# A hand-written order of 800 steps laid out anew around one shared port: attention and a two-layer network on one core

## The chip, the cores and the metric

The kernel runs on one core of a Trainium2 chip. The core has five engines with queues of their own: TensorE (PE, matmul; its weight loads are shown as PEld), VectorE (DVE), ScalarE (ACT), GpSimd (POOL) and SyncE (SP, which here issues all DMAs). The metric is the device time in microseconds (us); lower is better.

## The reference

Batch 4, 8 heads, 768 positions, head size 64. Each query sees the keys within 15 positions and, beside them, 24 block summaries (maximum of 32 keys, mean of 32 values, with log 32 added to the score). The result is the input of a network of two layers with a squared ReLU between them.

```python
k_sum = k.reshape(B, H, nb, block, D).max(axis=3)
v_sum = v.reshape(B, H, nb, block, D).mean(axis=3)
scores_l = scale * np.matmul(q, k.transpose(0, 1, 3, 2))
mask_l = np.abs(pos[:, None] - pos[None, :]) < window
scores_s = scale * np.einsum('bhsd,bhnd->bhsn', q, k_sum) + np.log(block)
scores_all = np.concatenate([np.where(mask_l, scores_l, -1e9), scores_s], axis=-1)
a = np.exp(scores_all - np.max(scores_all, axis=-1, keepdims=True))
a = a / (np.sum(a, axis=-1, keepdims=True) + 1e-09)
attn_out = np.matmul(a, np.concatenate([v, v_sum], axis=2))
...
x = attn_out.transpose(0, 2, 1, 3).reshape(B * S, H * D)   # 3072 x 512
h = np.maximum(x @ w_in, 0.0)                              # 512 -> 2048
return h * h @ w_out                                       # 2048 -> 512
```

## The kernel before

The attention is cut into 24 groups (4 batches x 6 tiles of 128 queries, all 8 heads), the network into 12 chunks of 256 rows, two groups each. The 2048 hidden units are 16 slices of 128; slice f has a weight tile that holds its part of both layers. Every float32 operand of the network is split into a rounded high part and a remainder (w high and low, xh and xl, gh and gl), and three products are added.

From chunk 2 on, a loop (`slot`, `period`) interleaves the network of one chunk with the attention of the next two groups. Ahead of it stands the head: groups 0 to 5, the whole preparation of the 16 weight tiles, and the network of chunks 0 and 1. The order of the head is written out by hand in the string `START`, one token for each step. The functions are called in the order of the tokens, so this string sets the order of the instructions in each engine's queue; the engines meet through semaphores. A token `TT2.5` means step TT for group 2, head 5; a letter at the end names the engine where there is a choice (a, v, p for ACT, DVE, POOL). The steps are:

- `L:x` a load on SP's queue (kv keys, q queries, vn and v values, w weights). Weight tile f goes into a room of the pool "w" (17 rooms, shared with keys and values), and its split copy w_sb takes another.
- `KS` block maxima (DVE); `S g.half` scores of four heads (PE, into banks 0 and 1 of PSUM); `TT` mask and maximum of one head (DVE); `E` exponential with its sum (ACT); `NR g.half` the inverse of four sums (DVE); `N` the multiplication by it (DVE or POOL); `T` transpose on PE, and `TC` its copy to SBUF.
- `SV` the block means of v on PE, `VC` their copies into the v tiles; `O g` outputs of group g (PE); `XH`, `XL` the split of x (ACT, DVE).
- For weight tile f: `HI` sign and scale (ACT), `LO` rounding (ACT or DVE), `SH` shift (DVE), `AD` add (POOL), `CA` high part (ACT or DVE), `SU` low part (DVE or POOL).
- `F1 u.j` a piece of the first layer (12 matmuls), `RE`, `SQ`, `MU`, `GL` the squared ReLU and its split (ACT or DVE, ACT, DVE, DVE), `F2 u.j` a piece of the second layer, `EV` the copy out. A unit u is a chunk and two slices; units 0 and 1 are chunk 0 with w0 to w3, units 2 to 5 chunk 1 with w0 to w7, and so on.
- `Wn`: n filler matmuls on zeros, whose results nobody reads.

The lines on which the steps rest: L164 KS, L263 S, L275 TT, L283 E, L293 and L296 NR, L301 N, L307 T, L110 every copy, L332 O, L346 and L349 XH and XL, L209 HI, L216 and L214 LO, L220 SH, L225 AD, L232 SU, L364 F1, L372 to L386 the squared ReLU, L410 F2, L543 fillers.

The mask-and-maximum reads scores from PSUM; the four sums of a half, `sm`, lie in SBUF.

Of the kernel before, what the change touches and what calls it, by code (L numbers as in the profile page):

```python
# [38 lines left out]


START = """
L:kv2 L:kv3 L:kv0 L:q0 L:mask L:kv1 L:w0 L:id L:q1 L:mean KS3 L:vn1 L:vn0 KS2 KS0 W7 S0.1 TT0.5 TT0.4 TT0.6 E0.4 TT0.7
KS1 E0.5 E0.7 E0.6 W3 S0.0 NR0.1 N0.1p L:q2 TT0.1 TT0.0 TT0.2 L:w1 E0.0 TT0.3 LO0v E0.1 L:v1 W3 T0.1 E0.3 L:v0 E0.2
S1.1 L:w2 HI0 NR0.0 S1.0 N0.0p TT1.4 TT1.7 TT1.6 TT1.5 E1.4 L:q3 SH0 E1.6 W1 T0.0 E1.7 AD0 TT1.1 TT1.2 TT1.0 E1.2
TC0.0v E1.0 E1.5 TT1.3 W6 SV E1.1 NR1.1 TC0.1v E1.3 N1.1p CA0a NR1.0 N1.0p S2.1 VC0v VC1a T1.1 VC2v SU0p VC3a T1.0
TC1.1a TT2.6 TT2.5 S2.0 TC1.0v HI1 L:q4 TT2.4 O1 TT2.0 TT2.7 E2.6 TT2.1 SH1 E2.7 O0 E2.0 LO1v E2.1 E2.5 L:v2 E2.4 CA1v
L:w3 XH1 NR2.1 AD1 L:w5 XH0 TT2.3 N2.1v L:v3 E2.3 L:w6 TT2.2 W8 T2.1 XL1 E2.2 L:w4 HI2 S3.0 NR2.0 SU1p N2.0v S3.1 LO2a
XL0 T2.0 L:q5 TT3.5 TT3.6 F1.0.0 E3.5 TT3.4 TT3.2 E3.6 TT3.7 TT3.0 E3.7 TT3.3 TT3.1 E3.4 SH2 S4.1 E3.3 NR3.1 E3.1 S4.0
AD2 TC2.1v E3.2 F1.0.1 E3.0 N3.1v CA2a NR3.0 TC2.0v N3.0p T3.1 HI3 SU2v O2 LO3a TC3.1v T3.0 SH3 RE0a F1.1.0 TC3.0a
TT4.6 AD3 MU0 SQ0 O3 TT4.7 GL0 E4.7 XH2 TT4.1 F2.0.0 TT4.4 XH3 CA3v LO6a TT4.0 SU3v F2.0.1 HI5 XL3 L:w11 F1.1.1 LO5a  # L50
L:v5 XL2 L:w7 TT4.2 L:w8 TT4.3 F1.3.0 TT4.5 RE1a L:w10 SH5 E4.3 L:v4 CA5v SQ1 L:w12 F1.2.0 AD5 MU1 E4.2 E4.4 GL1 E4.6
S5.0 E4.0 E4.5 S5.1 HI4 LO4v F1.3.1 HI6 SH4 SU5v AD4 F2.1.0 E4.1 CA4a NR4.1 F1.2.1 HI11 N4.1p SU4v HI7 F2.1.1 SH6
L:w15 L:w9 RE2a SH7 T4.1 AD6 MU2 F1.4.0 TC4.1a SQ2 RE3a GL2 F1.4.1 SQ3 NR4.0 MU3 N4.0p EV0.1a F1.6.0 GL3 RE4a LO7a
EV0.0v T4.0 CA6v HI10 F2.2.0 AD7 SU6v HI8 F2.2.1 LO8a SH11 F1.5.0 MU4 SQ4 CA7v LO10a F2.3.0 SU7v HI12 F2.3.1 SH8 HI9
CA8v F1.5.1 SH10 LO11a TC4.0v AD8 F1.6.1 GL4 F1.7.0 SH9 AD11 RE5v F1.7.1 SU8v SQ5 LO9a L:w13 F2.4.0 CA9v CA10a AD9
TT5.7 TT5.0 MU5 F2.4.1 HI15 GL5 RE6a AD10 O4 SU9v SQ6 F2.5.0 MU6 CA11a SU10v RE7a F1.8.0 SU11p LO12a GL6 L:w14 F2.5.1
MU7 HI13 SH15 F1.8.1 EV1.0a SH12 EV1.1a TT5.6 AD12 SQ7 TT5.3 F1.12.0 RE8a GL7 LO13a TT5.2 F2.6.0 CA12v HI14 TT5.1 MU8
F1.9.0 LO14a SH13 SH14 F1.9.1 E5.0 E5.7 SU12v AD13 F2.6.1 AD14 F2.7.0 SQ8 CA13a GL8 F2.7.1 TT5.5 TT5.4 E5.2 RE9v E5.3
SU13v LO15a F1.10.0 AD15 CA14a F2.8.0 E5.1 SU14v SQ9 F1.10.1 MU9 CA15a GL9 F2.8.1 E5.6 SU15v RE10a F1.11.0 SQ10 NR5.0
L:kw0 E5.5 N5.0v F1.11.1 MU10 F2.9.0 RE11a MU11 GL10 F2.9.1 VT0 F1.13.0 SQ11 E5.4 GL11 F1.12.1 KT0 NR5.1 L:kw1 N5.1v  # L60
F2.10.0 RE12v L:k6 MU12 F2.10.1 L:q7 L:q6 TU5.2 F1.15.0 SQ12 GL12 F1.13.1 KT1 VT1 F2.11.0 RE13a TU5.0 L:kw2 F2.11.1
F1.14.0 SQ13 EV2.1v TU5.1 F1.14.1 EV2.0v F1.15.1 MU13 GL13 RE14a F2.12.0 XH4 VT2 KT2 F2.12.1 MU14 L:kw3 F2.13.0 SQ14
XL4 L:k7 GL14 F2.13.1 RE15v MU15 F2.14.0 SQ15 GL15 F2.14.1 KT3 PK6a PK7a O5 S6.0 XH5 XL5 S6.1 VT3 S7.1 S7.0
"""


# [1 line left out]
def attn_ffn_kernel(ctx: ExitStack, tc: tile.TileContext, q, k, kt, v, vt, v0, w, masks, ident, mean, out):  # L68
    nc = tc.nc
# [36 lines left out]
    for t_ in [e_sb] + pT:
        nc.gpsimd.memset(t_, 0.0)

    def copy(eng, out, in_):
        nc.scalar.copy(out=out, in_=in_) if eng is nc.scalar else eng.tensor_copy(out=out, in_=in_)  # L110
# [125 lines left out]
    s_ps, nmx, sm = {}, {}, {}  # L236
# [51 lines left out]
            mask_max(g, h)  # L288
            exponentials(h)

    def inverse(half):

        nc.vector.scalar_tensor_tensor(  # L293
            out=sm[half], in0=sm[half], scalar=1.0e-9, in1=sm[half], op0=ALU.add, op1=ALU.max
        )
        nc.vector.reciprocal(sm[half], sm[half])  # L296
# [411 lines left out]
```

## Time and profile before

| | us |
|---|---|
| median of 3 runs (lowest, highest) | 622.37 (621.63, 623.36) |
| the profiled execution, its own time | 622.32 |
| its span in the trace | 620.5 |
| busy: PE, DVE, ACT, POOL | 601.2, 398.8, 264.4, 94.5 |
| granted TensorE clock over the span | 0.997 |

Rows of the profile name the line, the engine, the operation and the tiles, out<-in, with partitions x elements. In a timeline the first number is the start and the second the duration, and the bracket at the end says how long the engine idled before and what ended that. In a group, the numbers after the bar are the busy time of the group in us and the mean of one instruction in ns. A long run of the same instruction is one row (x64).

### The profile page before, as it was taken

The numbers are of one execution on the slowest core, as the hardware profiler recorded it, in microseconds if no ns is written. First come the engines' busy times: TensorE is split into PE (matmuls) and PEld (weight loads), VectorE is DVE, ScalarE is ACT, GpSimd is POOL, SyncE is SP. The second block draws the span as 40 slices with busy tenths as digits, with TensorE's granted clock in tenths as the row PEclk, the third lists the DMA queues.
The fourth block names the chain that finished last, engine by engine and source line by source line (L and its number), as shares of the span: only waits on it lengthen the run. The fifth ranks groups of instructions, "written<-read, shape, count | busy, mean of one in ns | idle before, by whom it ended". The sixth has DMA issues, their size and how long they took to land.

```text
span 620.5 us, 13086 instructions
## 1 busy us (share of the span) xinstructions
PE 601.2 (97%) x5300; PEld 539.9 (87%) x5300; DVE 398.8 (64%) x1044; ACT 264.4 (43%) x680; POOL 94.5 (15%) x83
## 2 busy tenths in 40 slices
...
GB/s 327 281 349 335 204 69 2 195 179 171 1 2 127 146 2 118 102 3 89 132 2 70 152 52 41 182 2 17 154 1 2 170 1 2 86 1 2 35 1 34
DMA packets 21868, 59.57 MB, mean 96 GB/s; under 512 B 2736, under 2 KB 2864, under 8 KB 19760
## 3 DMA queue, kind: packets, MB, share of 16 engines
...
q14 instruction: 19, 0.16, 0.1%
...
## 4 chain that ended last, share of the span: by engine, by line
PE 88%; DVE 4%; DMA 3%; ACT 2%; issue 1%; POOL 1%; SPq 1%; DVEq 0%; POOLq 0%; ACTq 0%
PE o_ps L410 40%; PE ph L364 38%; PE ph L332 3%; PE s_ps L247 2%; DMA v_sb<-in_v 2%; PE s_ps L364 2%; DVE w_sb L232 1%; PE s_ps L263 1%; DMA q_sb<-in_q 1%; ACT e_sb L283 1%; POOL e_sb L301 1%; PE ph L307 1%; DVE w_raw L220 0%; DVE sm L293 0%; DVE e_sb L301 0%
## 5 line engine op out<-in xcount | busy, mean ns | idle before, releaser
L364 PE MATMUL ph<-xh,w_sb 128*128 128x256 f32 x1408 | 247.3, 278 | 1.9 <-DVE gl L386 1.1
L410 PE MATMUL o_ps<-w_sb,gh 128*128 128x512 f32 x768 | 237.9, 391 | 0.0
L364 PEld LDWEIGHTS ph<-xh,w_sb 128*128 128x128 f32 x1408 | 217.9, 188 | 10.5 <-DVE gl L386 1.9
L364 PE MATMUL ph<-xl,w_sb 128*128 128x256 f32 x704 | 194.9, 277 | 0.0
L410 PEld LDWEIGHTS o_ps<-w_sb,gh 128*128 128x128 f32 x768 | 137.2, 188 | 24.9
L383 DVE TENSOR_TENSOR ph<-ph,r 128x512 f32<-128x512 f32 x88 | 61.4, 697 | 142.8 <-ACT r L372 142.3
L410 PE MATMUL o_ps<-w_sb,gl 128*128 128x512 f32 x384 | 151.3, 394 | 0.0
L372 ACT ACTIVATE r<-ph 128x512 f32<-128x512 f32 x85 | 50.5, 594 | 196.8 <-PE ph L364 193.3
L364 PEld LDWEIGHTS ph<-xl,w_sb 128*128 128x128 f32 x704 | 132.3, 188 | 0.0
L283 ACT ACTIVATE e_sb<-e_sb,nmx 128x120 f32<-128x120 f32 x192 | 73.7, 385 | 72.5 <-DVE nmx L275 72.5
L314 DVE STREAM_TRANSPOSE pT<-e_sb 32x256 f32<-32x256 f32 x228 | 99.3, 436 | 3.9 <-POOL e_sb L301 0.7
L301 POOL TENSOR_TENSOR e_sb<-e_sb,sm 128x480 f32<-128x480 f32 x43 | 43.2, 1006 | 322.8 <-DVE sm L296 180.1
L410 PEld LDWEIGHTS o_ps<-w_sb,gl 128*128 128x128 f32 x384 | 72.2, 188 | 14.5
L378 ACT ACTIVATE gh<-r 128x512 fp32r<-128x512 f32 x96 | 60.7, 632 | 20.3 <-PE o_ps L410 12.7
L386 DVE TENSOR_TENSOR gl<-ph,gh 128x512 fp32r<-128x512 f32 x88 | 60.9, 691 | 9.0 <-ACT gh L378 0.4
L275 DVE CUSTOM_DVE_ANT_0 e_sb<-s_ps,mask_sb 128x120 f32<-128x120 f32 x192 | 43.3, 277 | 3.3 <-PE s_ps L263 2.7
L225 POOL TENSOR_TENSOR w_raw<-w_raw 128x1024 int32<-128x1024 int32 x16 | 34.5, 2165 | 34.7 <-DVE w_raw L220 13.6
L283 ACT ACTIVATION_READ_ACCUMULATOR e_sb<-e_sb,nmx 128x1 f32 x192 | 36.1, 188 | 0.0
L349 DVE TENSOR_TENSOR xl<-ph,xh 128x512 fp32r<-128x512 f32 x20 | 13.7, 691 | 22.7 <-ACT xh L346 22.7
L293 DVE SCALAR_TENSOR_TENSOR sm<-sm 128x4 f32<-128x4 f32 x48 | 15.1, 314 | 17.2 <-ACT e_sb L283 17.2
L364 PE MATMUL s_ps<-xh,w_sb 128*128 128x256 f32 x128 | 24.1, 287 | 0.5 <-DVE w_sb L232 0.5
L232 DVE TENSOR_TENSOR w_sb<-w_raw,w_sb 128x1024 fp32r<-128x1024 f32 x13 | 22.0, 1696 | 1.7 <-ACT w_sb L110 1.3
...
## 6 DMA issues: line engine op xcount, KB each, us to landing
...
```

What stands on the lines that cost most here:

```text
L225: nc.gpsimd.tensor_tensor(out=lo, in0=hi, in1=lo, op=ALU.add)
L232: eng.tensor_sub(out=w_sb[f][:, 1], in0=words(f)[0].bitcast(F32), in1=w_sb[f][:, 0].bitcast(F32))
L275: nc.vector.tensor_tensor_reduce(out=e_sb[:, h, 0:NK], in0=s_ps[g][h % 2][:, h // 2, 0:NK], in1=m, scale=-scale, scalar=3.0e38, op0=ALU.ad ...
L283: nc.scalar.activation(e, e, AF.Exp, bias=nmx[half][:, i : i + 1], scale=-1.0, accum_out=sm[half][:, i : i + 1])
L301: eng.tensor_mul(out=e, in0=e, in1=sm[half].unsqueeze(2).to_broadcast([P, 4, NK]))
L314: nc.vector.transpose(out=pT[g % 2][j * 32 : j * 32 + 32, :, i * 32 : i * 32 + 32], in_=e_sb[i * 32 : i * 32 + 32, :, j * 32 : j * 32 + 32],)
L364: nc.tensor.matmul(ph, lhsT=w_sb[f][:, w, cc * P : (cc + 1) * P], rhs=x[c][:, cc, :], start=(n == 0), stop=(n == 3 * NC4 - 1))
L372: nc.scalar.activation(r, ph, AF.Relu)
L378: nc.scalar.activation(gh, r, AF.Square)
L383: nc.vector.tensor_mul(out=ph, in0=ph, in1=r)
L386: nc.vector.tensor_sub(out=gl, in0=ph, in1=gh.bitcast(F32))
L410: nc.tensor.matmul(o_ps[c][tt], lhsT=g_[:, ts_], rhs=w_sb[f][:, w, DM:], start=(first and n == 0), stop=(last and n == 2),)
```

## The change

- `START` is a new list for the whole head: other orders within every queue and other engines for some steps. The norms on POOL are 3 instead of 7 (on DVE 9 instead of 5), the low parts on POOL 5 instead of 3 (on DVE 11 instead of 13), the high parts on DVE 5 instead of 8. All four key loads stand ahead of q0. There are 31 fillers instead of 28, at other places.
- `inverse`: the sums' 1e-9 is added from four columns of bank 0 in PSUM (`eps`), so that only one operand lies in SBUF; where the norm runs on DVE, the inverse is written to four spare columns of bank 0, and the norm reads it there. The loop's inverses, whose norms run on POOL, get the new add alone.
- `place_v0` writes the means into one v tile, once; the new step `VP` (`spread_v0`) copies them from there to the other three places on POOL.
- An exponential on one column at the start makes ACT load its table of functions there. The zeroing of gh goes from POOL to DVE.

```diff
 START = """
-L:kv2 L:kv3 L:kv0 L:q0 L:mask L:kv1 L:w0 L:id L:q1 L:mean KS3 L:vn1 L:vn0 KS2 KS0 W7 S0.1 TT0.5 TT0.4 TT0.6 E0.4 TT0.7
...
+L:kv3 L:kv0 L:kv1 L:kv2 L:q0 L:mask L:w0 L:id L:q1 L:mean KS0 L:vn0 L:vn1 KS3 KS1 KS2 W12 S0.0 TT0.3 S0.1 TT0.0 E0.3
+TT0.2 E0.2 L:q2 TT0.6 TT0.7 E0.0 TT0.5 L:w1 TT0.1 E0.6 TT0.4 E0.1 E0.7 NR0.0p LO0v E0.4 E0.5 W10 S1.1 HI0 N0.0p NR0.1v
...
     nc.vector.memset(vsum, 0.0)
-    nc.gpsimd.memset(gh_sb.bitcast(F32), 0.0)
+
+    nc.scalar.activation(vsum[:, 0, 0:1], vsum[:, 0, 0:1], AF.Exp)
+    nc.vector.memset(bank[0][:, 3 * P + NK : 3 * P + NK + 4], 1.0e-9)
+    nc.vector.memset(gh_sb.bitcast(F32), 0.0)
...
     def place_v0(ps, j, eng):
-        for g in range(2):
-            copy(
-                eng, v_sb[g][96:128, :, j * P : (j + 1) * P],
-                ps[j * 32 : j * 32 + 32, 0:P].unsqueeze(1).to_broadcast([32, 2, P]),
-            )
+        copy(eng, v_sb[0][96:128, 0, j * P : (j + 1) * P], ps[j * 32 : j * 32 + 32, 0:P])
+
+    def spread_v0(j):
+        g, s = ((0, 1), (1, 0), (1, 1))[j]
+        nc.gpsimd.tensor_copy(out=v_sb[g][96:128, s, :], in_=v_sb[0][96:128, 0, :])
...
-    def inverse(half):
-
-        nc.vector.scalar_tensor_tensor(
-            out=sm[half], in0=sm[half], scalar=1.0e-9, in1=sm[half], op0=ALU.add, op1=ALU.max
-        )
-        nc.vector.reciprocal(sm[half], sm[half])
+    eps = bank[0][:, 3 * P + NK : 3 * P + NK + 4]
+
+    def inverse(half, eng=nc.gpsimd):
+        nc.vector.tensor_tensor(out=sm[half], in0=sm[half], in1=eps, op=ALU.add)
+        s = sm[half]
+        if eng is nc.vector:
+            sm[half] = bank[0][:, half * P + NK : half * P + NK + 4]
+        nc.vector.reciprocal(sm[half], s)
         del nmx[half]
...
+        elif op == "VP":
+            spread_v0(i)
...
-            inverse(j)
+            inverse(j, eng)
```

Three places show how the list moves instructions. The first is DVE's queue between the norm of group 2's second half and the first piece of the network. Before (sm_348 and sm_388 are the sums of group 2's second and first half, xl_448 the low part of x, s_ps_92 and s_ps_91 the outputs of groups 1 and 0):

```order
L301 TENSOR_TENSOR e_sb_79<-e_sb_79,sm_348 128x4x120
L275 ISA e_sb_79,nmx_387<-s_ps_89,mask_sb_70 128x120
L275 ISA nmx_387 128x1
L349 TENSOR_TENSOR xl_448<-s_ps_92,xh_421 128x4x128
L293 SCALAR_TENSOR_TENSOR sm_388<-sm_388 128x4
L296 RECIPROCAL sm_388<-sm_388 128x4
L301 TENSOR_TENSOR e_sb_79<-e_sb_79,sm_388 128x4x120
L349 TENSOR_TENSOR xl_448<-s_ps_91,xh_421 128x4x128
```

And now (sm_364 and sm_402 are the same two sums, s_ps_89 is bank 0, s_ps_91 and s_ps_92 the outputs):

```order
L300 TENSOR_TENSOR sm_364<-sm_364,s_ps_89 128x4
L304 RECIPROCAL s_ps_89<-sm_364 128x4
L279 ISA e_sb_79,nmx_401<-s_ps_90,mask_sb_70 128x120
L279 ISA nmx_401 128x1
L309 TENSOR_TENSOR e_sb_79<-e_sb_79,s_ps_89 128x4x120
L357 TENSOR_TENSOR xl_471<-s_ps_91,xh_444 128x4x128
L357 TENSOR_TENSOR xl_471<-s_ps_92,xh_444 128x4x128
L279 ISA e_sb_79,nmx_486<-s_ps_90,mask_sb_70 128x120
L279 ISA nmx_486 128x1
L300 TENSOR_TENSOR sm_402<-sm_402,s_ps_89 128x4
L304 RECIPROCAL s_ps_89<-sm_402 128x4
```

Both low parts of x have moved ahead of the inverse and the norm of group 2's first half, and the norm's second operand lies in PSUM.

The second place is POOL's queue at the same time. Before (w_raw_114, 189, 222 are w0 to w2, sm_516 a sum of group 3):

```order
L301 TENSOR_TENSOR e_sb_79<-e_sb_79,sm_245 128x4x120
L301 TENSOR_TENSOR e_sb_79<-e_sb_79,sm_262 128x4x120
L232 TENSOR_TENSOR w_sb_308<-w_raw_114,w_sb_308 128x1024
L225 TENSOR_TENSOR w_raw_189<-w_raw_189 128x1024
L232 TENSOR_TENSOR w_sb_417<-w_raw_189,w_sb_417 128x1024
L225 TENSOR_TENSOR w_raw_222<-w_raw_222 128x1024
L301 TENSOR_TENSOR e_sb_79<-e_sb_79,sm_516 128x4x120
```

And now (w_raw_116, 188, 333 are w0 to w2, sm_267 the sums of group 1's first half):

```order
L236 TENSOR_TENSOR w_sb_258<-w_raw_116,w_sb_258 128x1024
L309 TENSOR_TENSOR e_sb_79<-e_sb_79,sm_267 128x4x120
L148 COPY v_sb1_76<-v_sb0_75 32x512 x2
L148 COPY v_sb0_75<-v_sb0_75 32x512
L229 TENSOR_TENSOR w_raw_188<-w_raw_188 128x1024
L236 TENSOR_TENSOR w_sb_423<-w_raw_188,w_sb_423 128x1024
L229 TENSOR_TENSOR w_raw_333<-w_raw_333 128x1024
L236 TENSOR_TENSOR w_sb_582<-w_raw_333,w_sb_582 128x1024
```

One norm has left POOL here and w2's low part has come to it; the three copies of the means stand behind the remaining norm, and w0's low part ahead of it.

The third place is SP's queue after the loads of the means. Before (w_raw_189, 222, 419, 426 are w1, w2, w3, w5; q_sb1_78 takes q3, v_sb1_76 and v_sb0_75 take v1 and v0):

```order
L114 DMA q_sb0_77<-in_q 128x512
L198 DMA w_raw_189<-in_w 128x1024
L124 DMA v_sb1_76<-in_v 96x2x512
L124 DMA v_sb0_75<-in_v 96x2x512
L198 DMA w_raw_222<-in_w 128x1024
L114 DMA q_sb1_78<-in_q 128x512
```

And now (w_raw_188, 333, 377 are w1, w2, w3):

```order
L118 DMA q_sb0_77<-in_q 128x512
L202 DMA w_raw_188<-in_w 128x1024
L118 DMA q_sb1_78<-in_q 128x512
L128 DMA v_sb1_76<-in_v 96x2x512
L128 DMA v_sb0_75<-in_v 96x2x512
L202 DMA w_raw_333<-in_w 128x1024
```

q3 has moved ahead of v1, v0 and w2. Further on, nine weight tiles stand in one row (w4, w6, w7, w9, w13, w12, w8, w10, w11), where before two loads of v stood between them.

More of the change, by code (lines that the diff above doesn't have):

```diff
@@ L41 @@
 START = """
-L:kv2 L:kv3 L:kv0 L:q0 L:mask L:kv1 L:w0 L:id L:q1 L:mean KS3 L:vn1 L:vn0 KS2 KS0 W7 S0.1 TT0.5 TT0.4 TT0.6 E0.4 TT0.7
[L43 to L61, printed above, removed]
@@ L62 @@
-F1.14.0 SQ13 EV2.1v TU5.1 F1.14.1 EV2.0v F1.15.1 MU13 GL13 RE14a F2.12.0 XH4 VT2 KT2 F2.12.1 MU14 L:kw3 F2.13.0 SQ14
-XL4 L:k7 GL14 F2.13.1 RE15v MU15 F2.14.0 SQ15 GL15 F2.14.1 KT3 PK6a PK7a O5 S6.0 XH5 XL5 S6.1 VT3 S7.1 S7.0
+L:kv3 L:kv0 L:kv1 L:kv2 L:q0 L:mask L:w0 L:id L:q1 L:mean KS0 L:vn0 L:vn1 KS3 KS1 KS2 W12 S0.0 TT0.3 S0.1 TT0.0 E0.3
+TT0.2 E0.2 L:q2 TT0.6 TT0.7 E0.0 TT0.5 L:w1 TT0.1 E0.6 TT0.4 E0.1 E0.7 NR0.0p LO0v E0.4 E0.5 W10 S1.1 HI0 N0.0p NR0.1v
+N0.1v S1.0 SH0 T0.1 L:q3 L:v1 T0.0 CA0a AD0 TT1.4 TT1.7 L:v0 TT1.1 TC0.1v E1.1 E1.7 TT1.6 TT1.3 E1.6 TT1.5 SU0p W5 SV
```

20 lines of the change are left out of this document (added).

## The prediction

> **What bounds the kernel now.** I read the busy table in four stretches first, to see where TensorE (PE) is not full; then the chain that ended last in the poor stretch; then single VectorE (DVE) instructions there beside GpSimd's (POOL); then the loads.
>
> ```profile
> 0.00:40.00 40.00, 28.19 (x474) 22.31 (x475) 27.91 (x102) 22.80 (x78) 18.47 (x21) 0.96 0.91 307
> 40.00:140.00 100.00, 96.69 (x850) 85.89 (x850) 90.42 (x156) 60.50 (x102) 35.40 (x18) 1.00 0.50 179
> 140.00:600.00 460.00, 459.52 (x3882) 417.18 (x3881) 276.29 (x782) 176.23 (x494) 40.66 (x45) 1.00 0.19 63
> 600.00:620.50 20.50, 16.84 (x100) 14.53 (x98) 4.17 (x6) 4.86 (x8) 0.00 (x0) 1.00 0.07 26
> ```
>
> After the length of each stretch come busy PE, PEld, DVE, ACT and POOL, then clock, DMA share and GB/s. From 140 us on PE is full (459.5 of 460) until the tail. So only the head can pay: PE idles 11.8 us before 40 us and 3.3 us from 40 to 140, and some of its busy time there is the list's 28 filler matmuls. TensorE's useful work is the same in both kernels, so the end moves by what the head wins or loses.
>
> ```profile
> 25.25 2.08 PE L332 MATMUL s_ps<-pT,v_sb 128*64 128x64 f32 x64
> 27.26 2.10 PE L543 MATMUL o_ps<-gh 128*128 128x512 f32 x8
> 26.52 2.09 ACT e_sb L283 x11
> 28.64 1.42 DVE sm L293
> 30.43 2.59 DVE e_sb L301
> 33.16 0.63 PE ph L307 x4
> PE ph L307 <- DVE e_sb L301: 3.8, 1, 3.8
> 35.74 1.04 PE ph L307 x4
> 36.44 0.77 PE L364 MATMUL s_ps<-xh,w_sb 128*128 128x256 f32 x2
> 55.48 0.51 PE L364 MATMUL s_ps<-xh,w_sb 128*128 128x256 f32 x2
> ```
>
> Outputs O1 and O0 stand at 25.25; the first layer's first matmul (F1.0.0) stands at 36.44. Between them PE runs fillers, waits 3.8 us for a DVE norm, and does two transposes and group 3's scores. At 55.48 S5.1, the last scores of the head, has just ended.
>
> ```profile
> 28.64 1.41 DVE L293 SCALAR_TENSOR_TENSOR sm<-sm 128x4 f32<-128x4 f32 x1 [0.36 <-ACT e_sb L283]
> 30.35 2.66 DVE L301 TENSOR_TENSOR e_sb<-e_sb,sm 128x480 f32<-128x480 f32 x1
> 33.77 0.16 DVE L293 SCALAR_TENSOR_TENSOR sm<-sm 128x4 f32<-128x4 f32 x1
> 34.18 0.66 DVE L301 TENSOR_TENSOR e_sb<-e_sb,sm 128x480 f32<-128x480 f32 x1
> 27.75 2.27 POOL L225 TENSOR_TENSOR w_raw<-w_raw 128x1024 int32<-128x1024 int32 x1 [2.54 <-DVE w_raw L214]
> 30.10 2.39 POOL L232 TENSOR_TENSOR w_sb<-w_raw,w_sb 128x1024 fp32r<-128x1024 f32 x1
> ```
>
> The same add on four columns takes 0.16 alone and 1.41 beside POOL's add, the same norm 0.66 alone and 2.66 beside POOL's subtraction; both end as POOL's instruction ends. The groups say how much that is up to 110 us (x and mean ns), with an undisturbed one of the two largest and the last subtraction of the head:
>
> ```profile
> L232 DVE TENSOR_TENSOR w_sb<-w_raw,w_sb 128x1024 fp32r<-128x1024 f32 x13 | 22.0, 1696 | 1.7 <-ACT w_sb L110 1.3 <-POOL w_raw L225 0.2
> L220 DVE TENSOR_SCALAR w_raw<-w_raw 128x1024 int32<-128x1024 int32 x16 | 14.8, 941 | 1.7 <-ACT w_raw L209 1.6
> L301 DVE TENSOR_TENSOR e_sb<-e_sb,sm 128x480 f32<-128x480 f32 x4 | 5.7, 1434 | 0.1
> L293 DVE SCALAR_TENSOR_TENSOR sm<-sm 128x4 f32<-128x4 f32 x11 | 5.5, 502 | 2.9 <-ACT e_sb L283 2.9
> L383 DVE TENSOR_TENSOR s_ps<-s_ps,r 128x512 f32<-128x512 f32 x7 | 4.8, 688 | 0.2 <-ACT r L372 0.2
> 59.84 1.21 DVE L232 TENSOR_TENSOR w_sb<-w_raw,w_sb 128x1024 fp32r<-128x1024 f32 x1
> 26.38 0.70 DVE L220 TENSOR_SCALAR w_raw<-w_raw 128x1024 int32<-128x1024 int32 x1
> 106.84 1.22 DVE L232 TENSOR_TENSOR w_sb<-w_raw,w_sb 128x1024 fp32r<-128x1024 f32 x1
> ```
>
> Stretch: 13 x 0.49 + 16 x 0.24 + 4 x 0.77 + 11 x 0.34 = 17.0 us of DVE time. The multiply with one operand in PSUM (L383) has a mean of 0.69 and is not stretched; that is the form the change gives to the sums' add and to the norms on DVE.
>
> **The change, part by part.** Small edits first. The exponent's table is loaded at the start, so the first exponential no longer waits 1.28 for it; I credit that inside the walk below. The means take four copies instead of eight, and three POOL copies of 0.61 behind GpSimd's norm of group 1: they end before TC1.0 does, so nothing; without that cover they would cost 1.8. The fillers' memset goes to DVE, hidden in the wait for the first keys. The sums' add costs what it cost alone (0.16; with a PSUM operand at most the 0.69 of L383): 11 x 0.5 us is the worst for DVE over the head.
>
> ```profile
> 92.12 1.89 POOL L225 TENSOR_TENSOR w_raw<-w_raw 128x1024 int32<-128x1024 int32 x1 [1.29 <-DVE w_raw L220]
> L301 POOL TENSOR_TENSOR e_sb<-e_sb,sm 128x480 f32<-128x480 f32 x43 | 43.2, 1006 | 322.8 <-DVE sm L296 180.1 <-ACT e_sb L283 140.1 <-ACT gh L378 2.0
> L186 POOL COPY v_sb<-v_sb 32x512 f32<-32x512 f32 x3 | 1.8, 613 | 0.0
> L209 ACT ACTIVATE w_raw<-w_raw 128x1024 f32<-128x1024 f32 x16 | 18.0, 1152 | 0.0
> 9.98 1.28 ACT L283 ACT_TABLE_LOAD   x1 [9.98 <-DVE nmx L275]
> 2.10 5.73 DMA q_sb<-in_q
> 16.94 0.66 PE L307 MATMUL s_ps<-id_sb,e_sb 128*128 128x128 f32 x4
> 11.96 1.65 PE L543 MATMUL o_ps<-gh 128*128 128x512 f32 x3
> 17.35 1.63 PE L543 MATMUL o_ps<-gh 128*128 128x512 f32 x6
> DMA packets 5287, 19.29 MB, mean 321 GB/s; under 512 B 1023, under 2 KB 1151, under 8 KB 3836
> ```
>
> The list I walk, adding durations of these rows.
>
> Step 1, to the end of T0.0. All four key loads now stand ahead of q0, which landed at 7.83: 0.39 MB more at 0.321 MB/us puts it at 9.1. Two halves of scores, ten fillers, S1.1; NR0.1 waits for S1.1 (both touch bank 0), then its inverse and DVE norm, 1.0, S1.0 and T0.1, T0.0. Fillers took 0.55 each at 11.96 (half clock) and 0.27 at 17.35. At the fast rate T0.0 ends at 15.9, at the slow one at 19.0; before it was 17.6. I take 17.0: twelve fillers now run ahead of the scores, not seven, and before the rate rose after about 6 us of work. [...] The two filler rows agree that there are two rates.
>
> Step 2, T0.0 to F1.0.0. Start of group 1's exponentials 0.5; eight of them 3.15 (11 instructions in 2.09, so 0.38 each); inverse 0.4; POOL's norm 1.1; T1.0 0.45; copy 0.9 with its place in DVE's queue; O1 and O0 2.1 (64 matmuls, 2.08); then on DVE inverse 0.35, the norm N2.1 0.66, two low halves of x 1.2, steps between them 0.3. Sum 11.1: F1.0.0 at 28.1, against 36.44. What went is the 1.25 + 2.0 of stretch, the eight fillers with the wait behind them (most of 5.9), and group 3's first half and T2.0 no longer in between. Loads fit: v0's last byte is the 7.4th MB, at 23.0.
>
> Step 3, F1.0.0 to the end of S5.1. Both lists have then done six first-layer and two second-layer pieces and groups 0 to 3's outputs. Before: 55.48 - 36.44 = 19.0. After: the same work, T2.0 more, two fillers, and a new wait of about 1.3 for SU2, now on POOL (2.39 instead of 1.21, behind an add of 1.9); against that stand waits of before, since 19.0 is no row of work alone. I take 19.1, an estimate that can err by 1.5 either way: S5.1 ends at 47.2, a lead of 8.3.
>
> Step 4, from there on. Before, PE lost 3.3 us in 40 to 140. Now it asks for each weight 8 us sooner. The list moves to POOL two subtractions net and takes four norms from it; three casts go from DVE to ACT (1.1 each, hidden there while ACT is not late). In port time (POOL's work plus DVE's stretchable work) the head's total falls by 4 x 1.0 for POOL's norms, 5 x 0.66 for DVE's, 3 x 0.7 casts and 11 x 0.16 adds, and rises by 2 x (2.39 - 1.21) and 3 x 0.61: 7.0 less. If the port alone paced the last weights and freed time counted one to one, they would come 7.0 sooner, and 1.3 of 8.3 would go back. I take 1.5.
>
> Sum: 8.3 - 1.5 = 6.8 us less. The profiled execution took 622.32 (span 620.5 and 1.8 around it), 0.05 below the median of the runs: **615.5**.
>
> **The rivals.** One: the lead is kept whole, and the 3.3 us of small waits shrink as well. DVE's 17.0 us of stretch speak for it; ACT's 60.5 busy us of the 100, now wanted in some 8 less, against. Gain 9 to 11, about 612.
>
> Two: most of the lead is given back to the loads. By the list w8 is the 19.1th MB; at 0.321 it lands at 59.5, and ACT comes to its sign step at about 60: 47.2 and then seven passes over weights of 1.1, seven exponentials and five small steps of 0.5. All of ACT's later list waits behind it. Three slices of this row, from 36 us (1.5 us each), show 258 to 272 while the queue is full:
>
> ```profile
> GB/s 0 240 324 232 352 456 408 397 414 437 423 434 269 259 234 330 363 102 149 292 306 322 328 411 258 261 272 437 393 442 339 142 187 348 393 437 421 404 343 298
> ```
>
> At 0.265 from 37 us on, w8 lands near 64.4, ACT stands 4.6, and the gain is 3 to 4: about 619.
>
> Three, no change: the stretch was hidden by PE's queue of ready work, or returns because shift, cast and subtraction still meet POOL. The 3.8 us wait of PE on the stretched norm speaks against the first. [...] What stays is 16 x (1.89 + 0.70) + 11 x 1.21 + 5 x 2.39 + 8 casts and roundings x 0.7, three norms and three copies: 77 us of port time against 84. Before, the 84 lay between 13 us and the end of the last subtraction at 108, 95 us; packed as well, 77 take 87 and end at 100, 8 us sooner. For no change the packing would have to fall from 0.88 to 0.81.
>
> Four, slower: the same ACT stall, deeper. w13 now loads ahead of w12 and w8. From the point where w8 lands after about 70 the ACT stall of 10 us eats the lead and the 1.9 us beyond it: 7.25 MB in 33 us, 0.22 MB/us. Lower slices (102, 142) stand only where the queue ran empty; if w8's room comes free late, that returns. About 625.
>
> **How the numbers follow.** A change within 0.3% (1.9 us) can't be told from none here. Forecast (gain 4.5 to 9) 0.55; rival one 0.12; rival two (1.9 to 4.5) 0.15; rival three 0.09; rival four 0.09. Faster is 0.55 + 0.12 + 0.15 = 0.82, within 0.09, slower 0.09. The range takes T0.0 at 15.9 and most of rival one at its lower end (611.5) and reaches through rival two into rival three above (620.0).
>
> **What would show it.** First layer starting at 27 to 30 and S5.1 ending at 46 to 49 show steps 1 to 3; the sums' add at 0.2 or less in every place, and no DVE norm above 0.8, show the port term; PE idle between 47 and 130 of 4 to 5 us shows step 4. I would be wrong if S1.1 or O0 starts late for a load, if a wait between scores and inverses in bank 0 repeats per group, or if ACT stands for w8 or w12.

## The result, and the profile after

| | before | after |
|---|---|---|
| median (lowest, highest), us | 622.0 (621.26, 623.36), 4 runs | 615.49 (613.61, 616.38), 4 runs |
| ratio after/before, 95% interval | | 0.9889 [0.986, 0.9918] |
| profiled execution; its span | 622.32; 620.5 | 613.61; 611.8 |

The change wins 6.5 us of the medians (1.0%), more than the 0.3% that can be told from nothing. The profiled execution of after is its fastest: the granted clock over its span is 1.00, in the other three 0.993 to 0.994, and their spans are 613.6 to 614.6. So 8.7 us lie between the two profiled spans and 6.5 between the medians; the difference goes with the lower clock.

The busy table of after, in the same columns as before (length; busy PE, PEld, DVE, ACT, POOL; clock, DMA share, GB/s):

```profile
0.00:40.00 40.00, 30.59 (x553) 24.80 (x554) 28.15 (x110) 25.86 (x82) 20.45 (x22) 1.00 0.91 321
40.00:140.00 100.00, 100.00 (x837) 90.22 (x837) 82.88 (x174) 62.15 (x114) 34.21 (x19) 1.00 0.54 194
140.00:600.00 460.00, 459.52 (x3873) 416.87 (x3872) 270.18 (x763) 174.17 (x480) 39.15 (x43) 1.00 0.18 58
600.00:611.80 11.80, 8.05 (x47) 6.71 (x45) 1.39 (x2) 2.40 (x4) 0.00 (x0) 1.00 0.11 44
```

PE idles 9.4 us before 40 us instead of 11.8, and not at all from 40 to 140, where it lost 3.3. That is 5.7 us. The other 3.1 is busy time: PE is busy 598.2 us instead of 601.2 with the same useful work. Before, the granted clock was 0.83 between 30 and 40 us, right behind the 3.8 us wait for the held norm; after, it is 1.00 in every stretch.

The groups of VectorE up to 110 us (count, busy us, mean ns):

```profile
L236 DVE TENSOR_TENSOR w_sb<-w_raw,w_sb 128x1024 fp32r<-128x1024 f32 x11 | 14.2, 1294 | 0.5 <-ACT w_sb L114 0.4
L224 DVE TENSOR_SCALAR w_raw<-w_raw 128x1024 int32<-128x1024 int32 x16 | 12.6, 796 | 0.9 <-ACT w_raw L213 0.9
L309 DVE TENSOR_TENSOR e_sb<-e_sb,s_ps 128x480 f32<-128x480 f32 x9 | 5.9, 651 | 0.2
L300 DVE TENSOR_TENSOR sm<-sm,s_ps 128x4 f32<-128x4 f32 x12 | 1.9, 155 | 3.0 <-PE s_ps L267 2.0 <-ACT e_sb L287 1.1
```

The add has a mean of 0.155 (0.50 before), the norm 0.65 (1.43), the low part 1.29 (1.70), the shift 0.80 (0.94). The 17.0 us of stretch before are now some 2.5: 11 x 0.08 for the low parts and 16 x 0.10 for the shifts.

One date says how long the head took in each kernel. From chunk 2 on both kernels do the same steps at the same pace, and in each of these periods there is one block of 64 output matmuls in one go (the first is O6 and O7). In the chain of waits (start, duration, what), before:

```profile
178.25 2.02 PE ph L332 x64
```

and after:

```profile
169.45 2.02 PE ph L340 x64
```

In both, the next such block follows 47.94 us later, and so on to the end. So the head ends 8.8 us sooner, and nothing behind it changes. I call the date of the first such block the mark.

### The profile page after: what moved, and what is told of

Its sections match the earlier page's. It is cut to its first block, busy times and chain, and to the rows that moved or that the text cites. A ratio compares the mean times of both kernels' runs of the same rounds, so it can differ in the third digit from the quotient of the medians.

```text
span 611.8 us, 13094 instructions
## 1 busy us (share of the span) xinstructions
PE 598.2 (98%) x5303; PEld 538.6 (88%) x5303; DVE 382.6 (63%) x1047; ACT 264.6 (43%) x678; POOL 93.8 (15%) x83
## 4 chain that ended last, share of the span: by engine, by line
PE 95%; DVE 1%; ACT 1%; DMA 1%; issue 0%; SPq 0%; DVEq 0%
PE o_ps L418 43%; PE ph L372 40%; PE s_ps L372 4%; PE ph L340 3%; PE s_ps L251 3%; PE s_ps L267 1%; DMA q_sb<-in_q 1%; ACT e_sb L287 1%; PE s_ps L340 1%; DVE e_sb L279 0%; PE s_ps L315 0%; DVE e_sb L309 0%; DVE pT L114 0%; SPq L160 0%; PE ph L315 0%
## 5 line engine op out<-in xcount | busy, mean ns | idle before, releaser
L418 PEld LDWEIGHTS o_ps<-w_sb,gh 128*128 128x128 f32 x768 | 137.2, 188 | 24.9
L309 POOL TENSOR_TENSOR e_sb<-e_sb,sm 128x480 f32<-128x480 f32 x39 | 38.5, 995 | 324.0 <-DVE sm L304 182.1
L229 POOL TENSOR_TENSOR w_raw<-w_raw 128x1024 int32<-128x1024 int32 x16 | 33.0, 2072 | 32.0 <-ACT w_raw L220 15.7
L354 ACT CAST xh<-ph 128x512 fp32r<-128x512 f32 x21 | 12.3, 586 | 31.9 <-PE ph L340 31.9
L340 PEld LDWEIGHTS ph<-pT,v_sb 128*64 128x64 f32 x672 | 20.6, 138 | 4.1 <-issue 3.6
L372 PE MATMUL s_ps<-xh,w_sb 128*128 128x256 f32 x128 | 22.6, 279 | 0.0
```

The costliest lines, as they stand in the source:

```text
L229: nc.gpsimd.tensor_tensor(out=lo, in0=hi, in1=lo, op=ALU.add)
L309: eng.tensor_mul(out=e, in0=e, in1=sm[half].unsqueeze(2).to_broadcast([P, 4, NK]))
L340: nc.tensor.matmul(xp[o : o + 64, h // 2, s * 64 : s * 64 + 64], lhsT=v_sb[g % 2][:, s, h * 64 : h * 64 + 64], rhs=pT[g % 2][:, h, s * 64 ...
L372: nc.tensor.matmul(ph, lhsT=w_sb[f][:, w, cc * P : (cc + 1) * P], rhs=x[c][:, cc, :], start=(n == 0), stop=(n == 3 * NC4 - 1))
L418: nc.tensor.matmul(o_ps[c][tt], lhsT=g_[:, ts_], rhs=w_sb[f][:, w, DM:], start=(first and n == 0), stop=(last and n == 2),)
```

## Which part carries it

Two lists (475 tokens before, 477 after; the 800 of the title is too high) and two inverses make four kernels. The small edits go with the list: the copies of the means, the zeroing of gh and the early exponential. Only the last of them was also tried alone. "The port" is only a name for what the rows show, VectorE instructions that last longer beside GpSimd's: the adds 0.50 and the norms 1.43 us on average before, 0.155 and 0.65 with one input in PSUM. This kernel has the new list and the old inverse:

```diff
...
-        nc.vector.tensor_tensor(out=sm[half], in0=sm[half], in1=eps, op=ALU.add)
-        s = sm[half]
-        if eng is nc.vector:
-            sm[half] = bank[0][:, half * P + NK : half * P + NK + 4]
-        nc.vector.reciprocal(sm[half], s)
+        nc.vector.scalar_tensor_tensor(
+            out=sm[half], in0=sm[half], scalar=1.0e-9, in1=sm[half], op0=ALU.add, op1=ALU.max
+        )
+        nc.vector.reciprocal(sm[half], sm[half])
```

> The new list with the inverse of the kernel before: sums, their add (scalar_tensor_tensor) and their inverses all in SBUF, nothing of them in bank 0. Theory (the port): the eleven adds and nine VectorE norms of the head meet GpSimd again, the adds stand at a mean of 0.3 to 0.5 us instead of 0.16 and the norms at 0.9 or more instead of 0.65, and since PE waits for these norms the time is 3 to 7 us above the changed kernel, 618.5 to 622. Rival (the order alone): the list already keeps the users of the port apart, adds stay under 0.2 and norms under 0.75, the false waits through bank 0 (1.27 and 0.87 us before S1.0 and S2.1) go, and the time is 613.5 to 616.

Measured: 623.4 us, ratio to before 1.0001 [0.9981, 1.0022]. The list alone is worth nothing. Its groups of adds and VectorE norms up to 110 us:

```profile
L298 DVE SCALAR_TENSOR_TENSOR sm<-sm 128x4 f32<-128x4 f32 x11 | 9.7, 880 | 1.3 <-ACT e_sb L286 1.3
L306 DVE TENSOR_TENSOR e_sb<-e_sb,sm 128x480 f32<-128x480 f32 x8 | 9.4, 1174 | 0.2
```

Its chain, at the add and the norm ahead of F1.0.0, and at the mark:

```profile
28.25 1.58 DVE sm L298
30.22 2.60 DVE e_sb L306
179.25 2.02 PE ph L337 x64
```

In this list the old add is held longer than in the old list (0.88 against 0.50 on average), add and norm are again links of the chain, and the mark is later than before the change. The port theory stands, with the adds and the time above its ranges; the rival (613.5 to 616) is out.

The other half: the old list, with the new inverse as in the change. Each `NR` in it takes the letter of its norm, here the first of twelve:

```diff
-NR0.1 N0.1p
+NR0.1p N0.1p
...
-            inverse(j)
+            inverse(j, eng)
```

> The list of the kernel before with the new inverse alone (add from a PSUM column, inverses for VectorE's norms in bank 0). Theory (the port on the path): the stretched add and norm ahead of F1.0.0 (1.25 and 2.0 us too long) are gone, F1.0.0 starts 2 to 4 us sooner than 36.4, and the time is 617 to 620. Rival (order alone): the stretch moves to other instructions of this list or becomes new waits through bank 0, F1.0.0 stands within 1 us of 36.4, and the time is 621 to 624.

Measured: 620.3 us, ratio 0.996 [0.9945, 0.9975], a gain of 2.6. The adds are 0.154 and the norms 0.65, but F1.0.0 starts at 35.4, only 1.0 sooner. The timeline shows what took the place of the held norm:

```profile
32.48 0.16 DVE L295 TENSOR_TENSOR sm<-sm,s_ps 128x4 f32<-128x4 f32 x1 [0.78 <-PE s_ps L264]
33.60 0.45 PE L264 MATMUL s_ps<-kv,q_sb 64*64 64x96 f32 x8 [1.24 <-DVE e_sb L304]
```

The add waits for scores, then scores wait for the norm: both touch bank 0 now, and each waits for the other though their columns differ. PE idles 2.5 us from 40 to 140 us here, where it idled 3.3 before and 3.3 with the list alone (e1). So neither theory is whole: the stretch goes, and part of it comes back through the bank. New inverse alone 2.6, list alone 0, both 6.5: some 4 us come only from the two together.

Which of the two operations was it, the add or the norm? First the norm alone put back: the inverse stays in SBUF, the add still reads PSUM (`s` and the reciprocal's input are then `sm[half]` itself).

```diff
-        if eng is nc.vector:
-            sm[half] = bank[0][:, half * P + NK : half * P + NK + 4]
```

> The changed kernel with all inverses left in SBUF: the add still reads eps from PSUM, the VectorE norms have two SBUF inputs. Theory (norms carry it): the nine VectorE norms of the head stand at a mean of 0.9 to 1.2 us instead of 0.65, PE waits for them ahead of S2.1, T2.1, T2.0 and T4.0, and the time is 617.5 to 620. Rival (the add carries it, and it is one small instruction that holds up the list): norms longer by 0.2 at most, time 614.5 to 616.5.

The group of the norms up to 110 us, and the mark in the chain:

```profile
L307 DVE TENSOR_TENSOR e_sb<-e_sb,sm 128x480 f32<-128x480 f32 x9 | 11.4, 1268 | 0.2
```

```profile
169.40 2.02 PE ph L338 x64
```

Measured: 614.5 us (613.4 to 615.6), ratio 0.9871 [0.985, 0.9892]. Here the theory falls: the norms are held as it said (mean 1.27, twice their length), and the time is that of the changed kernel. The rival is right in the time, and wrong in the norms' length. In the profiled run S0.0 started 1.25 us sooner than in that of the changed kernel (q0's load) and the mark is the same, so the held norms may cost about 1 us; the medians do not show it.

Then the add alone put back, with eps in an SBUF tile:

```diff
-    nc.vector.memset(bank[0][:, 3 * P + NK : 3 * P + NK + 4], 1.0e-9)
+    eps = const.tile([P, 4], F32, name="eps")
+    nc.vector.memset(eps, 1.0e-9)
...
-    eps = bank[0][:, 3 * P + NK : 3 * P + NK + 4]
```

> The changed kernel with the eps of the sums' add in SBUF, so that this add (tensor_tensor, four columns) has no operand in PSUM; inverses and norms as in the changed kernel. Theory (an operation with two SBUF inputs is held by GpSimd, and PE waits for these sums): the twelve adds of the head have a mean of 0.5 to 0.9 us instead of 0.16, some of them over 1.2, and the time is 618 to 621: of the 7.9 us that the list loses with the old inverse, half or more. Rival (four columns are too short to be held, the norms were it): adds under 0.25, time 614.5 to 616.

Measured: 627.1 us, ratio 1.0065 [1.0048, 1.0082]: slower than before. The adds up to 110 us:

```profile
L300 DVE TENSOR_TENSOR sm<-sm,eps 128x4 f32<-128x4 f32 x12 | 9.4, 780 | 1.4 <-ACT e_sb L288 1.4
```

In the timeline, the add ahead of F1.0.0, and the scores that wait for the norm behind it:

```profile
29.31 1.65 DVE L300 TENSOR_TENSOR sm<-sm,eps 128x4 f32<-128x4 f32 x1
31.99 0.60 PE L268 MATMUL s_ps<-kv,q_sb 64*64 64x96 f32 x8 [2.78 <-DVE e_sb L309]
```

The busy table there (the third figure from the end is the clock):

```profile
28.00:32.00 4.00, 1.22 (x44) 1.08 (x41) 3.93 (x10) 3.71 (x16) 3.22 (x2) 0.93 0.89 305
32.00:36.00 4.00, 4.00 (x43) 3.75 (x44) 2.71 (x12) 1.60 (x4) 1.45 (x1) 0.50 0.87 314
36.00:40.00 4.00, 4.00 (x52) 3.71 (x51) 2.29 (x11) 2.02 (x7) 1.89 (x1) 0.71 1.04 324
```

Its chain, at the mark and at one later block of twelve second-layer matmuls:

```profile
178.49 2.02 PE ph L340 x64
304.15 2.80 PE o_ps L418 x12
```

Such a block in the chain of the changed kernel:

```profile
305.03 2.75 PE o_ps L418 x12
```

The mark is 9.0 us later than in the changed kernel, nearly as much as with the whole old inverse (9.8). The other 3.9 of the 12.9 us between the profiled spans are another thing, which neither theory had: behind the mark the steady period is 48.37 us instead of 47.94, since twelve second-layer matmuls take 2.80 instead of 2.75. Nine periods of 0.43 make the 3.9. The same slower matmuls stand ahead of the mark too: 264 of them, or 22 blocks of twelve, at 0.05 each some 1.1 of the 9.0, an estimate. That leaves about 8 for the held adds. So of the two it is the add of four columns that decides, and the theory holds on the add, though the time lies above its range. As for the slower matmuls: this kernel has a tile of 16 bytes more in SBUF. In the run with the old inverse, whose adds also have all operands in SBUF but which has no such tile, the period is 47.94; that it is the tile that slows the matmuls is still an inference, and how it would, no run shows.

Why the small operation and not the large one? The add is ahead of the inverse and the norm, so these two start only behind it, and it ended at 30.96 where GpSimd's add ended at 30.94: here the norm ended 2.6 us after its add began. With the norm held, add and inverse run meanwhile: 2.15 in the run above. Free, it is 1.1 (27.71 to 28.83 in the changed kernel). The held add is worse by 0.5 at this place, and PE, standing 2.78, also lost its clock. That such places add up to the 8 us is argued, not shown. Both kinds are held in these runs with two SBUF inputs (adds 0.50, 0.88 and 0.78 on average, norms 1.43, 1.17 and 1.27), and neither with one in PSUM (0.15 to 0.16 and 0.65); which of the two kinds costs this kernel time, only the two runs with one of them put back say.

## The wait costs clock as well

That is the second part of the price. After the wait, 0.50 and 0.71 of the clock: F1.0.0's twelve matmuls took 2.56 instead of 1.42. The same kernel, with fillers inside the wait:

```diff
-N2.1v S3.0 XH0
+N2.1v W8 S3.0 XH0
```

> The kernel with eps in SBUF (627.1 us) with eight more filler matmuls on PE between O0 and S3.0, that is inside the 2.78 us for which PE stands there for the norm behind the held add. Nothing of the data's order changes. In that kernel the granted clock after this wait was 0.50 from 32 to 36 us and 0.71 from 36 to 40, and F1.0.0's twelve matmuls took 2.56 instead of 1.42. Theory (the wait's larger part is the clock that it costs): PE stays at 1.00 from 32 to 40, F1.0.0's twelve take about 1.4, and the time falls by 2 to 3.5 us, to 623.5 to 625, though the add is as long as before. Rival (the half rate has another cause, or the fillers only take the wait's place): clock and time as they were, 626 to 627.9.

The busy table at the same place and at the next wait, and the mark in the chain:

```profile
28.00:32.00 4.00, 4.00 (x99) 3.64 (x89) 3.60 (x10) 3.98 (x14) 2.04 (x1) 1.00 0.83 298
32.00:36.00 4.00, 3.43 (x51) 2.84 (x51) 3.66 (x14) 2.34 (x8) 2.63 (x2) 1.00 0.84 267
36.00:40.00 4.00, 4.00 (x82) 3.67 (x83) 3.97 (x18) 3.97 (x14) 1.89 (x1) 1.00 1.01 268
44.00:48.00 4.00, 3.92 (x32) 3.83 (x34) 3.59 (x15) 2.17 (x3) 2.38 (x2) 0.59 1.02 426
```

```profile
178.21 2.02 PE ph L340 x64
```

Measured: 625.0 us, ratio 1.004 [1.0021, 1.0059]; the intervals just overlap with those without the fillers. The add is as long as it was (1.58 in both chains), the clock holds at 1.00 and F1.0.0 runs as in the changed kernel (its first two matmuls 0.40, without the fillers 0.63). In this profiled run T0.0 ended 1.3 later than in the other and the mark is 0.3 sooner, so from T0.0 on it is 1.6 better; the medians say 2.1 and the ratios to the kernel before 1.6, with runs from 622.4 to 628.0, so the size is rough. Behind the next wait for a held add (1.86 us at 42) the clock was 0.59; without the fillers it was 1.00 there, behind a wait of 1.91. The theory holds for the clock, and its gain comes out at the low end of its range or a little under it: of the 8 us of the held adds some 1.6 to 2.1 are the clock behind one wait.

The start of the kernel has the same trouble, and here the number of fillers made no clear difference. Three instead of ten behind the first scores:

```diff
-E0.5 W10 S1.1
+E0.5 W3 S1.1
```

> The changed kernel with three fillers instead of ten between S0.1 and S1.1 (W3 for W10). In runs of this list the ten took 2.6 us where the clock had risen and 4.0 to 4.1 where it had not. Theory (in most runs they stand on the path): S1.1 moves up by 1 to 2.5 us to where its own data are ready (group 0's maxima are taken by 13.0), T0.0 ends 0.5 to 1 us sooner, and the time falls by 0.3 to 1 us. Rival (the clock needs them): PE falls back to half rate for more of the stretch up to 30 us, T0.0 gains nothing and F1.0.0 comes later, the time grows by 0.5 to 2 us.

Measured: 614.5 us (614.2 to 615.0), ratio 0.9866 [0.9849, 0.9883]: neither theory is whole. S1.1 came at 14.3, against 15.2 with ten fillers at half rate, but PE ran at 0.50 from 12 to 20 us and T0.0 ended at 20.0, which is later and not sooner. The median is 1.0 below that of the changed kernel, as the theory asked, but the intervals overlap, and the earlier T0.0 that was to give the gain did not come.

## What step 2 missed

The prediction's walk to F1.0.0 was 2.8 us short. The trace of after, in the order of time (T0.1 and T0.0, waits at bank 0, the gap ahead of O0, F1.0.0, and F2.1.0 right behind S5.1):

```profile
15.95 0.40 PE L267 MATMUL s_ps<-kv,q_sb 64*64 64x96 f32 x8 [1.27 <-DVE e_sb L309]
16.64 1.09 PE L315 MATMUL s_ps<-id_sb,e_sb 128*128 128x128 f32 x8
21.21 0.40 PE L267 MATMUL s_ps<-kv,q_sb 64*64 64x96 f32 x8 [0.87 <-DVE e_sb L309]
22.09 0.16 DVE L300 TENSOR_TENSOR sm<-sm,s_ps 128x4 f32<-128x4 f32 x1 [0.93 <-PE s_ps L267]
28.19 1.15 PE L340 MATMUL s_ps<-pT,v_sb 128*64 128x64 f32 x32 [1.51 <-issue]
30.91 0.40 PE L372 MATMUL ph<-xh,w_sb 128*128 128x256 f32 x2
38.00 0.16 DVE L300 TENSOR_TENSOR sm<-sm,s_ps 128x4 f32<-128x4 f32 x1 [1.05 <-PE s_ps L267]
51.04 0.74 PE L418 MATMUL o_ps<-w_sb,gh 128*128 128x512 f32 x2
```

The bank first. No run here drops these waits, so what would come without them is not shown. What can be done is to use a bank in which no scores land. For groups 0 to 3 the eps column and the inverses go to unused columns of the bank that takes the means:

```diff
+    idle = [ps_o.tile([P, DM], F32, name="o_ps")]
+    spare = ps_o.tile([P, DM], F32, name="o_ps")
+    nc.vector.memset(spare[:, P : P + 4], 1.0e-9)
...
-        nc.vector.tensor_tensor(out=sm[half], in0=sm[half], in1=eps, op=ALU.add)
+        nc.vector.tensor_tensor(out=sm[half], in0=sm[half], in1=spare[:, P : P + 4] if g < 4 else eps, op=ALU.add)
...
+            o = P + 4 + half * 4
-            sm[half] = bank[0][:, half * P + NK : half * P + NK + 4]
+            sm[half] = spare[:, o : o + 4] if g < 4 else bank[0][:, half * P + NK : half * P + NK + 4]
```

> The changed kernel, with the eps column and the inverses of groups 0 to 3 moved from bank 0 to unused columns of the bank that receives the means, which no scores touch. Theory (the shared bank is what step 2 missed): S1.0 and S2.1 no longer wait for norms (1.27 and 0.87 us), the adds no longer wait for scores (0.93 and 1.05 us), F1.0.0 stands 1.5 to 2.5 us sooner than in the other runs of this list (30.9 and 31.7 to 31.9 us), and the time falls by 1 to 2 us, to 613.5 to 614.5. Rival (those waits stood beside others): PE finds the next wait right behind, F1.0.0 moves by less than 0.7 and the time stays at 615 to 616.

F1.0.0 in its timeline, and the mark in its chain:

```profile
30.75 0.40 PE L376 MATMUL ph<-xh,w_sb 128*128 128x256 f32 x2
```

```profile
168.70 2.02 PE ph L344 x64
```

Measured: 612.8 us (612.4 to 613.2), ratio 0.9838 [0.9821, 0.9855], an interval wholly below that of the changed kernel. It is the best version of all: by the medians 2.7 us below the changed kernel, and 1.6% below before. The three other runs of this list with eps and the inverses in bank 0 (three fillers, v1 and v0 first, no early exponential) have medians of 614.4 to 615.3, so 1.6 to 2.7 is what the runs bear out. No scores wait for a norm up to 40 us in its trace. In its profiled run the ten fillers took 4.3 us, and F1.0.0 is still 0.8 to 1.0 sooner than in two other runs of this list where they took 4.0 to 4.1 (31.5 and 31.7). The theory holds in the time, beyond its range; at F1.0.0 it gives less than it said.

The gap ahead of O0, 1.51 us with no releaser in the trace. Is it v0, which SP issues only behind q3 (16.8 us)?

```diff
-TT0.5 L:w1 TT0.1
+TT0.5 L:w1 L:v1 L:v0 TT0.1
...
-S1.0 SH0 T0.1 L:q3 L:v1 T0.0 CA0a AD0 TT1.4 TT1.7 L:v0 TT1.1
+S1.0 SH0 T0.1 L:q3 T0.0 CA0a AD0 TT1.4 TT1.7 TT1.1
```

> The changed kernel with the loads v1 and v0 ahead of q3 in SyncE's queue, which holds q3 until S1.0 has ended (16.8 us). Theory (v0's load is late): the 1.5 us that PE stands before O0 go, O1 is followed by O0 at once, F1.0.0 stands at 29.0 to 29.7 instead of 30.9, and the time is 0.5 to 1.5 us less. Rival (what PE stands for is its own instructions): the gap of about 1.5 us stays at O0 or comes at another place before 32 us, F1.0.0 at 30.5 to 31, the time unchanged within 0.4.

Measured: 615.3 us (614.0 to 615.4), ratio 0.9872 [0.9855, 0.9889]: no change. The gap at O0 is gone, but now group 3's second half of scores, which stand ahead of O1 in PE's queue, wait for q3. Its chain has that load:

```profile
17.61 8.09 DMA q_sb<-in_q
```

F1.0.0 came at 31.5 with the ten fillers at half rate. The rival's outcome (a gap at another place, the time unchanged) came, though not for its reason: here PE waited for the next load in the queue. And the 1.51 was not v0: by the profile of the changed kernel v0's load was issued at 17.6 and landed 7.3 later, at 24.9, and O0 began at 28.19. In four other runs of this list the wait ahead of O0 ended with an exponential on ACT (0.44 us with the old inverse, 2.23 with the inverses in SBUF, 0.66 with the columns apart, 1.16 with q0 ahead as well). That the 1.51 is the same wait is likely, and not shown.

No attempt to start sooner gained time. With the columns apart, and q0's load ahead of kv2's:

```diff
-L:kv3 L:kv0 L:kv1 L:kv2 L:q0 L:mask
+L:kv3 L:kv0 L:kv1 L:q0 L:kv2 L:mask
```

> The kernel with eps and inverses apart from the scores' bank (612.8 us) with the load of q0 ahead of that of kv2. Theory (step 1 is set by q0, the last of five loads): q0 lands 0.7 to 1 us sooner, S0.0 starts at about 8.2 instead of 9.06, S0.1 still waits for the sums of kv2 until about 10, and the time falls by 0.3 to 0.9 us, to 612 to 612.5. Rival (GpSimd, ACT and the later loads set the head by then): S0.0 sooner, but F1.0.0 and the time within 0.3 us.

Measured: 613.2 us (612.0 to 613.6), ratio 0.9842 [0.9821, 0.9863]. S0.0 started at 7.2, 1.9 us sooner and more than the theory asked; O1 then waited 1.1 for v1, and F1.0.0 came at 30.9, 0.15 later than without it. The rival is right, though the time is 0.4 up and not within 0.3. With eighteen fillers ahead of the first scores instead:

```diff
-KS2 W12 S0.0
+KS2 W18 S0.0
```

> The kernel with eps and inverses apart from the scores' bank (612.8 us) with eighteen fillers instead of twelve ahead of the first scores, so that PE has no gap of 2.25 us between the fillers and q0. In that kernel's profiled run the clock was 0.63 from 8 to 12 us and 0.52 from 12 to 16, and the ten fillers behind the scores took 4.26. Theory (the gap costs the clock): the clock is 1.00 from 8 to 16 in the profiled run, the ten fillers take 2.6 to 2.7, and the time falls by 0.5 to 1.5 us. Rival (the clock's start is set by something else, or T0.0 waits for other work by then): clock as before, or full and the time within 0.4 us.

Measured: 613.1 us (611.6 to 615.8), ratio 0.9852 [0.9825, 0.9878]. In the profile the clock is 1.00 up to 24 us and the ten fillers take 2.50, as the theory says; the time has not moved, as the rival says. Group 3's scores and O1 wait for loads again (0.87 and 0.55), and the clock falls then. The load in the chain of the first of these two:

```profile
14.25 9.96 DMA v_sb<-in_v
```

The stretch behind it in the busy table of the second:

```profile
24.00:28.00 4.00, 3.33 (x75) 3.13 (x77) 3.14 (x14) 2.73 (x9) 1.95 (x2) 0.62 1.00 372
```

Last, fillers in these gaps, on top of q0 ahead of kv2:

```diff
-TT2.3 O1 TT2.2 SH1 E2.6 CA1v O0
+TT2.3 W4 O1 TT2.2 SH1 E2.6 CA1v W4 O0
```

> The kernel with eps and inverses apart from the scores' bank and q0 ahead of kv2 (613.2 us, 612.0 to 613.6), with four fillers ahead of O1 and four ahead of O0. In that kernel's profile PE stood 1.08 us for v1 ahead of O1 and 1.16 for ACT ahead of O0, and the granted clock was 0.87 from 24 to 28 us and 0.71 from 28 to 32. Theory (short waits in a row cost the clock): the fillers lie in the gaps, the clock is 1.00 from 24 to 32, and the time falls by 0.8 to 1.7 us, to 611.5 to 612.4, which would be the fastest of all. Rival (PE has slack there or the fillers push O1 and O0 back): 613 to 614.

Its timeline of PE there:

```profile
24.15 0.40 PE L270 MATMUL s_ps<-kv,q_sb 64*64 64x96 f32 x8 [1.31 <-DMA q_sb<-in_q]
24.84 2.08 PE L554 MATMUL o_ps<-gh 128*128 128x512 f32 x4
```

Measured: 614.1 us (613.7 to 614.5), ratio 0.9861 [0.9845, 0.9878], against 613.2 without them. A miss: this time the gap came ahead of the scores, where no filler stood, and the four fillers behind it ran at half rate (2.08) and pushed O1 back. The rival's half on being pushed back is what happened.

The last small part is the exponent's table:

```diff
-    nc.scalar.activation(vsum[:, 0, 0:1], vsum[:, 0, 0:1], AF.Exp)
```

> The changed kernel without the one early exponential that loads ACT's table. Theory: the load of 1.28 us returns in front of the first real exponential, on the path to T0.0, and the time is 0.8 to 1.3 us above the changed kernel. Rival: the ten fillers behind the first scores cover it, S1.1 and T0.0 stand within 0.3 us of where they stood, and the time is the same within 0.4.

Measured: 614.4 us (614.0 to 615.8), ratio 0.9866 [0.9848, 0.9884]; mark 169.97. But this run does not test the price of a late load: its table load still stood at 0.73 us, as in the changed kernel, and not at 9.98 as before:

```profile
0.73 1.28 ACT L286 ACT_TABLE_LOAD   x1 [0.73 <-PEq L707]
```

The early exponential adds nothing here, and it is not what makes ACT load the table at the start; what moved the load is open.

## Why the prediction was right, point by point

The sum was right (615.5 forecast, 615.49 measured), and two of its terms were not. That they offset each other is luck. Of the prediction's own signs, the port term's came, and those for steps 1 to 4 did not: F1.0.0 at 30.9 (27 to 30 asked), the end of S5.1 at 51.0 (46 to 49), PE idle from 47 to 130 us 0 (4 to 5). One of its signs of being wrong came as well: waits between scores and inverses in bank 0 that repeat.

- **The port term** was right in mechanism and in what goes: adds at 0.16 in every place, no norm above 0.66. In the changed kernel the other forms still last longer at places beside GpSimd's adds: a shift 2.38 (0.68 at least), a low part 2.04 (1.22), a rounding 1.09 (0.66). One reading was loose: the norm of 2.66 did not end as GpSimd's subtraction ended (32.49) but 0.52 later (33.01), about its own length. And the prediction counted add and norm alike (1.25 + 2.0 in step 2). The runs with one of them put back show that the add carries it: about 8 us at the mark for the held adds, and about 1 at most for the held norms alone. With both held (the old inverse) it is 9.8.
- **Step 1** (T0.0 at 17.0) was 0.7 short: 17.7 in the profiled run, 18.6 to 18.9 in runs of this list where the ten fillers took 4.05 to 4.15. Both lie inside the ends that the prediction gave (15.9 and 19.0), and both rates of the fillers occur, from run to run of one list. What sets the rate of a run is open.
- **Step 2** (11.1 us, F1.0.0 at 28.1) was the first term mis-sized: 13.2, F1.0.0 at 30.9. It priced the waits through bank 0 once (NR0.1, in step 1) and took O0 as following O1 at once. The bank waits came at four places up to 38 us, two of them in this step (0.87 and 0.93); with the columns apart 1.6 to 2.7 us of the time go. The 1.51 ahead of O0 is the other part. "v0 at 23.0" left out that SP's queue stops at q3 until S1.0 has ended, and v0 landed at 24.9, but that is not what O0 waited for. Eight exponentials at 0.38 are 3.04, not 3.15; this changes little.
- **Step 3** (19.1 us) took 20.1, inside its stated error. The lead at the end of S5.1 was 4.4, not 8.3.
- **Step 4** had the wrong sign. It gave 1.5 back to the port's pace; instead 4.4 us more were won between S5.1 and the mark. The busy table over 84.5 us from that place, before:

```profile
55.48:140.00 84.52, 81.69 (x627) 72.04 (x621) 76.75 (x122) 47.73 (x75) 29.83 (x14) 1.00 0.42 147
```

  and after:

```profile
51.04:135.56 84.52, 84.52 (x655) 76.11 (x650) 70.12 (x133) 50.56 (x96) 24.82 (x13) 1.00 0.47 165
```

  PE's idle 2.8 us there are gone, with VectorE 6.6 us less busy. That is the mechanism of rival one (the small waits shrink with the stretch), which had 0.12. It takes both parts of the change: from 40 to 140 us PE idles 3.3 with the new list and the old inverse, 2.5 with the old list and the new inverse, and not at all with both. Some 1.5 of the 4.4 are busy time of PE. Of these, 0.9 lie in the same 480 first-layer matmuls (59.5 us busy before, 58.6 after) and 0.4 in the same 64 scores at the end of the list (2.3 and 1.9); why these are shorter is open.
- **What was left out**: the clock. Before, PE's wait of 3.8 us was followed by a clock of 0.77 and 0.81 from 32 to 40 us (1.7 us of array time), and the rows quoted there showed it (F1.0.0's first two matmuls 0.77, later ones 0.51). The prediction priced the wait, not the half rate behind it.
- **Rivals two and four** (ACT stands for w8 or w12) did not come: from 40 to 60 us the loads moved 404 to 431 GB/s, not 265, and PE never waited.

The mis-sized terms (3.9 too much lead, 5.9 too little behind it) offset each other to within 2 us in the profiled pair; the other runs of the changed kernel, at a lower clock, are 1.8 to 2.8 longer. That the sum fits does not confirm the walk; only the port term and the place where PE idles were confirmed one by one.
